# Window attention in front of a saturated TensorE: scores and products with v as float32 matmuls on parts of the array

## Chip, cores and metric

One core of a Trainium2 chip runs the whole program. The metric is device time in microseconds (us) of one execution. The profile's engines are PE (TensorE matmul), PEld (its weight loads), DVE (VectorE), ACT (ScalarE), POOL (GpSimd) and SP (SyncE, whose queue issues all DMAs here).

## What is computed

```python
# batch 8, heads 8, seq 576, head_dim 64; d_model 512, d_ff 2048; all inputs and the output float32
scores = scale * q @ k.T                       # masked to 0 <= i - j < 64
attn   = softmax(scores); a = attn @ v         # per batch and head
x      = a laid out as (4608 tokens, 512)
h      = x @ w_in
out    = (max(h, 0) + log1p(exp(-abs(h)))) @ w_out
```

Every token attends to itself and the 63 tokens before it.

## The kernel before, in words

The 4608 tokens are cut into 12 blocks of 384 (`TB`). In each block, attention is done for four pairs of heads (`hp`), and then the feed-forward part runs over 16 slices `f` of 128 of the 2048 inner columns. One step of the feed-forward part is an "up" (`ffn_up`, 12 matmuls at L390 into a bank `ps_h`, of which there are two) and a "down" (`ffn_down`, 9 matmuls at L411 into three accumulating banks `ps_o`). Matmul operands there are float32r pairs: a rounded part and the remainder, three products for each exact one. After an up, ACT takes abs, exp and ln (L394 to L396) and DVE adds the positive part and splits the result (L398 to L401).

`attention(g, hp)` is a generator. Each `yield` ends a stage, and the tables `STG0` (blocks 0 and 1) and `STG` (later blocks) give each stage a place on a common scale on which step n has its up at 2n + 0.5 and its down at 2n + 5.5. All events are sorted by that place. PE executes them exactly in this order (`MANUAL`); the other engines get their order from a scheduler, and each then works through its own queue in order. In later blocks a new pair of heads begins every 8 places, so every four feed-forward steps.

There are two kinds of attention:

- Blocks 0 and 1 (`by_pe`, eight pairs of heads) use plain float32. The scores of 128 queries for both heads come from one matmul against a block-diagonal tile `kbd` (L263). The probabilities are turned by PE (L303), and the products with v (L352) are 12 matmuls, 64 columns of v as the weight and 64 queries streamed, first the six of one head, then the six of the other; the two heads write different halves of the output's partitions.
- The ten later blocks (40 pairs) split q and k into float32r parts on ACT and DVE (L241, L242, L247, L248): the scores take 4 matmuls for 128 queries (L267). The probabilities are split into two float16 parts `nat`, turned by two transposing DMAs into `tr` (L311). v is split into three bfloat16 parts (L331 to L335), and 18 matmuls for each head (L364) multiply. DVE and ACT add the two halves of the result (L370, L371) and split it into `x` (L373, L374).

The scores cover 192 keys for 128 queries; the first and the last 64 columns hold a query's window in the upper and the lower half of the partitions. L274 scales, masks and takes the minimum, and L280 folds the last 64 columns onto the first. ACT takes exp (L284), and L293 and L295 normalise. Attention's banks are three `ps_a`.

At the start, the weights arrive as raw words and are rebuilt by ACT and DVE (`load_w`, L176 to L183), while attention of the first blocks runs beside it.

Of the kernel before, what the change touches and what calls it, by code (L numbers as in the profile page):

```python
# [17 lines left out]
P = 128  # L18
# [13 lines left out]
STG = (-13, -5.9, -5, 0, 1, 2, 3, 4, 5, 6, 7, 7.1, 12, 14, 16, 17)  # L32
# [11 lines left out]
def window_attention_softplus_ffn(  # L44
# [70 lines left out]
    W = CH + P  # L115

    kbd_s = [att.tile([P, 2, CH + TB], F32, name="kbd", tag=f"k{i}") for i in range(2)]
    for t in kbd_s:  # L120
        nc.vector.memset(t[D:P, 0, :], 0.0)
        nc.vector.memset(t[0:D, 1, :], 0.0)
        nc.vector.memset(t[0:D, 0, 0:CH], 0.0)
        nc.vector.memset(t[D:P, 1, 0:CH], 0.0)

    v3z = cpool.tile([P, 2, NJ, 2, 2, D], BF16, name="v3z")
    v_ts = [att.tile([P, 2, NJ, P], F32, name="v_t", tag=n) for n in ("nat", "tr")]
    for t in v_ts:
        nc.vector.memset(t[0:CH, 0, 0, :], 0.0)
# [4 lines left out]
    mask = cpool.tile([P, W], BF16, name="mask")  # L134
    nc.gpsimd.memset(mask, 0.0)
    nc.gpsimd.affine_select(
        out=mask, in_=mask, pattern=[[1, W]], compare_op=ALU.is_gt, fill=FAR, base=0, channel_multiplier=-1
    )
    nc.gpsimd.affine_select(
        out=mask, in_=mask, pattern=[[-1, W]], compare_op=ALU.is_ge, fill=FAR, base=CH, channel_multiplier=1  # L140
    )

    mask_c = cpool.tile([P, W], BF16, name="mask_c")
    nc.gpsimd.tensor_copy(mask_c, mask)
    nc.gpsimd.memset(mask_c[:, 0:CH], FAR)
    ident = att.tile([P, P], F32, name="ident", tag="xf")
    make_identity(nc, ident)

    mask_b = cpool.tile([P, W], BF16, name="mask_b")
    nc.gpsimd.tensor_copy(mask_b, mask)  # L150
    nc.gpsimd.memset(mask_b[CH:P, 0:P], FAR)
    nc.gpsimd.memset(v3z, 0.0)
# [3 lines left out]
    def load_w(f):  # L156


        if f < NE + 4:
            k = FIRST[f % 4] if f < NE else (4, 6)[f % 2]  # L160
            parts = [(spare(k, [P, 2, DM], w_words.dtype, "raws"), spare(k + 1, [P, 2, DM], F32, "ws"), 0, 2)]
        else:
            parts = [
                (
                    ff.tile([P, 1, DM], w_words.dtype, name="raw"),
                    att.tile([P, 1, DM], F32, name="wh", tag=("v_in", "v12")[m]),
                    m, m + 1,
                )
                for m in range(2)
            ]  # L170
# [18 lines left out]
    def attention(g, hp):  # L189
# [12 lines left out]
        heads = [slice(0, D), slice(D, P)]  # L202

        if by_pe:
            qf = ld.tile([P, 2, TB], F32, name="q_in") if hp % 2 else ld.tile([P, 2, W - P + TB], F32, name="k_in")
            qf = qf[:, 0, 0:TB]
            kf = kbd_s[hp % 2]
            skip = CH if t0 == 0 else 0
            nc.sync.dma_start(qf, qT[c0 : c0 + P, t0 : t0 + TB])
            for hh in range(2):  # L210
                nc.sync.dma_start(kf[heads[hh], hh, skip:], kT[c0 + hh * D : c0 + (hh + 1) * D, t0 - CH + skip : t0 + TB])
        else:
            q_in = ld.tile([P, 2, TB], F32, name="q_in")
            k_in = ld.tile([P, 2, W - P + TB], F32, name="k_in")
            ts, ks = slice(t0, t0 + TB), slice(t0 - CH, t0 + TB)
            for half in heads:
                nc.sync.dma_start(
                    q_in[half, :, :], qT[c0 : c0 + P, ts].rearrange("(h d) t -> d h t", h=2)
                )
                nc.sync.dma_start(  # L220
                    k_in[half, :, :], kT[c0 : c0 + P, ks].rearrange("(h d) t -> d h t", h=2)
                )
        yield

        if by_pe:
            v_t = v_ts[hp % 2]

            def load_v(rows, lay, j0, j1, start):
                n = rows.stop - rows.start
                src = v[start + j0 * P : start + j1 * P, c0 : c0 + P].rearrange("(j p) n -> p j n", p=P)  # L230
                nc.sync.dma_start(v_t[rows, lay, j0:j1, :], src[:n, :, :])

            if t0 == 0:
                nc.sync.dma_start(v_t[CH:P, 0, 0, :], v[0:CH, c0 : c0 + P])
            load_v(slice(0, P), 0, 1 if t0 == 0 else 0, NJ, t0 - CH)
            load_v(slice(0, CH), 1, 0, NJ, t0 + CH)
            load_v(slice(CH, P), 1, 0, NJ, t0)
        else:
            q_hl = att.tile([P, 2, TB], F32R, name="q_hl")
            low = heads[1]  # L240
            nc.scalar.copy(q_hl, q_in)  # L241
            nc.vector.tensor_tensor(  # L242
                q_hl[low, :, :], q_in[low, :, :], q_hl[low, :, :].bitcast(F32), ALU.subtract
            )
            yield
            k_hi, k_lo = [att.tile([P, 2, W - P + TB], F32R, name=f"k{i}") for i in range(2)]
            nc.scalar.copy(k_hi, k_in)  # L247
            nc.vector.tensor_tensor(k_lo, k_in, k_hi.bitcast(F32), ALU.subtract)  # L248
        yield

        if g == 0:

            st = spare(FIRST[hp], [P, 2, NJ, W], F32, "st0")
        else:
            st = att.tile([P, 2, NJ, W], F32, name="st", bufs=2)
        mn = att.tile([P, 2, NJ], F32, name="mn", bufs=2)
        sm = att.tile([P, 2 * NJ], F32, name="sm", bufs=2)
        for j in range(NJ):
            sp = bank()
            spv = sp[:, : 2 * W].rearrange("p (h c) -> p h c", h=2)  # L260
            js, kc = slice(j * P, (j + 1) * P), slice(j * P, j * P + W)
            if by_pe:
                mm(spv, qf[:, js], kf[:, :, kc], start=True, stop=True)  # L263
            else:
                for hh in range(2):
                    for i, part in enumerate((k_hi, k_lo)):
                        mm(  # L267
                            spv[:, hh, :], q_hl[:, hh, js], part[:, hh, kc],
                            start=(hh == 0 and i == 0), stop=(hh == 1 and i == 1), skip_group_check=True,
                        )  # L270
            t = ORDER[g] * NJ + j
            m = mask_c if (t * P) % S == 0 else mask_b if (t * P) % S + P > S else mask
            for hh in range(2):
                nc.vector.tensor_tensor_reduce(  # L274
                    st[:, hh, j, :], spv[:, hh, :], m, QSCALE, 3.0e38, ALU.add, ALU.min, mn[:, hh, j : j + 1]
                )
            yield

        sv = st.rearrange("p h j c -> p (h j) c")
        nc.vector.tensor_tensor(sv[:, :, 0:CH], sv[:, :, 0:CH], sv[:, :, P:], ALU.min)  # L280
        for hh in range(2):
            for j in range(NJ):
                i = hh * NJ + j
                nc.scalar.activation(  # L284
                    sv[:, i, 0:P], sv[:, i, 0:P], AF.Exp, bias=mn[:, hh, j : j + 1], scale=-1.0, accum_out=sm[:, i : i + 1]
                )
# [7 lines left out]
        pn = sv[:, :, 0:P]  # L294
        nc.vector.tensor_tensor(pn, pn, sm.unsqueeze(2).to_broadcast([P, 2 * NJ, P]), ALU.mult)  # L295
        if by_pe:

            yield
            pt = att.tile([P, 2, TB], F32, name="pt", tag="q_hl")
            for hh in range(2):  # L300
                pp = bank()
                for j in range(NJ):
                    tp(pp[:, j * P : (j + 1) * P], sv[:, hh * NJ + j, 0:P], ident)  # L303
                nc.scalar.copy(pt[:, hh, :], pp[:, :TB])
        else:
# [8 lines left out]
            nc.scalar.copy(nat[:, 0, :, :], pn)  # L314
            turn(0)
            yield
            nc.vector.tensor_tensor(nat[:, 1, :, :], pn, nat[:, 0, :, :], ALU.subtract)
            turn(1)
            yield
            v_in = att.tile([P, 2, NJ, P], F32, name="v_in")  # L320

            before, own = [v[t : t + TB, c0 : c0 + P].rearrange("(j p) n -> p j n", p=P) for t in (t0 - CH, t0)]
            nc.sync.dma_start(v_in[:, 0, :, :], before)
            nc.sync.dma_start(v_in[0:CH, 1, :, :], own[CH:P, :, :])
            nc.sync.dma_start(v_in[CH:P, 1, :, :], own[0:CH, :, :])
            yield

            v12 = att.tile([P, 2, NJ, 2, 2, D], BF16, name="v12")
            vv = v_in.rearrange("p u j (h d) -> p (u j h) d", h=2)
            v1, v2, v3 = [t.rearrange("p u j h i d -> p (u j h) i d")[:, :, i, :] for t, i in ((v12, 0), (v12, 1), (v3z, 0))]  # L330
            nc.scalar.copy(v1, vv)  # L331
            nc.vector.tensor_tensor(vv, vv, v1, ALU.subtract)
            yield
            nc.scalar.copy(v2, vv)
            nc.vector.tensor_tensor(v3, vv, v2, ALU.subtract)  # L335
# [8 lines left out]
        if by_pe:  # L344
            av = bank()
        else:
            xf = att.tile([P, TB], F32, name="xf")
        for hh in range(2):
            if by_pe:
                for a in range(2 * NJ):  # L350
                    cs = slice(a * CH, (a + 1) * CH)
                    mm(  # L352
# [159 lines left out]
```

## Time and profile before

| | |
|---|---|
| median of three runs | 1008.7 us (1007.8 to 1010.62) |
| the profiled execution, its span | 1013.1 us, 1011.3 us |
| PE matmul | 959.9 us, 6240 instructions |
| PE weight loads | 851.7 us |
| DVE | 730.4 us, 1689 instructions |
| ACT | 710.4 us, 1673 instructions |
| DMA queue of the program | 99.65 MB, 36.8% of 16 engines' span |

Busy time of PE is time in which some matmul is under way. A matmul's record begins at its start and ends when its results have left the array, so records of a stream overlap, and the pace of a stream is read from start to start, not from one record's length. A float32 matmul (L263, L352) leaves two weight loads and two matmul records; a float32r, bfloat16 or float16 one leaves one of each. In the chain of waits a piece's length is the time until the next piece takes over.

### The profile page before, as it was taken

The numbers are of one execution on the slowest core, as the hardware profiler recorded it, in microseconds if no ns is written. First come the engines' busy times: TensorE is split into PE (matmuls) and PEld (weight loads), VectorE is DVE, ScalarE is ACT, GpSimd is POOL, SyncE is SP. The second block draws the span as 40 slices with busy tenths as digits, with TensorE's granted clock in tenths as the row PEclk, the third lists the DMA queues.
The fourth block names the chain that finished last, engine by engine and source line by source line (L and its number), as shares of the span: only waits on it lengthen the run. The fifth ranks groups of instructions, "written<-read, shape, count | busy, mean of one in ns | idle before, by whom it ended". The sixth has DMA issues, their size and how long they took to land.

```text
span 1011.3 us, 17290 instructions
## 1 busy us (share of the span) xinstructions
PE 959.9 (95%) x6240; PEld 851.7 (84%) x6240; DVE 730.4 (72%) x1689; ACT 710.4 (70%) x1673; POOL 3.7 (0%) x14
## 2 busy tenths in 40 slices
PE   6546999999999999999999999999999999999998
PEld 3335888898988998899899998899889989998997
DVE  6897588787777777787777777777768867864332
ACT  4566678787777777777777677777767767865443
POOL 1000000000000000000000000000000000000000
PEclk9767999999999999999999999999999999999999
DMA  5845234443333434333334344433423423410000
GB/s 171 292 164 174 90 125 115 128 116 102 92 99 82 110 86 98 101 91 103 97 83 113 99 82 99 112 74 91 129 70 90 134 66 82 112 32 17 32 1 32
DMA packets 137238, 100.76 MB, mean 100 GB/s; under 512 B 70080, under 2 KB 129216, under 8 KB 135616
## 3 DMA queue, kind: packets, MB, share of 16 engines
q1 hardware_dynamic: 137152, 99.65, 36.8%
q8 instruction: 49, 0.80, 0.3%
q14 instruction: 37, 0.30, 0.1%
HBM read 73.66 MB, written 10.22 MB: 83 GB/s over the span
## 4 chain that ended last, share of the span: by engine, by line
PE 85%; DMA 6%; DVE 4%; ACT 4%; issue 1%; SPq 0%; ACTq 0%; DVEq 0%
PE ps_h L390 37%; PE ps_o L411 36%; PE ps_a L267 5%; PE ps_a L364 4%; DMA raws<-in_w_words_dram 3%; DMA raw<-in_w_words_dram 2%; ACT st L284 1%; DVE ws L178 1%; PE ps_a L263 1%; ACT ws L176 1%; PE ps_a L352 1%; DVE w L183 0%; DVE st L295 0%; DMA k_in<-in_kT_dram 0%; DVE ws L179 0%
## 5 line engine op out<-in xcount | busy, mean ns | idle before, releaser
L390 PE MATMUL ps_h<-x,w 128*128 128x384 f32 x2304 | 440.0, 339 | 0.6 <-ACT x L373 0.4
L411 PE MATMUL ps_o<-w,g 128*128 128x512 f32 x1728 | 433.9, 395 | 4.3 <-DVE g L401 3.1
L390 PEld LDWEIGHTS ps_h<-x,w 128*128 128x128 f32 x2304 | 404.7, 189 | 11.9 <-DVE u L398 1.0
L411 PEld LDWEIGHTS ps_o<-w,g 128*128 128x128 f32 x1728 | 319.5, 189 | 65.5 <-DVE g L401 5.2
L394 ACT ACTIVATE u<-ps_h 128x384 f32<-128x384 f32 x192 | 94.3, 491 | 198.3 <-PE ps_h L390 191.6
L398 DVE SCALAR_TENSOR_TENSOR u<-ps_h,u 128x384 f32<-128x384 f32 x192 | 106.9, 557 | 112.0 <-ACT u L396 109.3
L401 DVE TENSOR_TENSOR g<-u,g 128x384 fp32r<-128x384 f32 x192 | 106.3, 554 | 27.2 <-ACT g L400 25.9
L284 ACT ACTIVATE st<-st,mn 128x128 f32<-128x128 f32 x288 | 111.4, 388 | 9.4 <-DVE st L280 9.3
L274 DVE CUSTOM_DVE_ANT_0 st<-ps_a,mask 128x192 f32<-128x192 f32 x216 | 68.5, 351 | 50.5 <-PE ps_a L267 49.6
L395 ACT ACTIVATE u<-u 128x384 f32<-128x384 f32 x192 | 100.8, 525 | 4.4
L396 ACT ACTIVATE u<-u 128x384 f32<-128x384 f32 x192 | 100.2, 522 | 4.2
L400 ACT CAST g<-u 128x384 fp32r<-128x384 f32 x112 | 57.3, 512 | 31.9 <-DVE u L398 31.5
L267 PE MATMUL ps_a<-k,q_hl 128*128 128x192 f32 x480 | 76.6, 282 | 0.0
L267 PEld LDWEIGHTS ps_a<-k,q_hl 128*128 128x128 f32 x480 | 66.5, 191 | 3.2
L364 PEld LDWEIGHTS <-v 128*128 128x128 bf16 x960 | 44.1, 98 | 17.3 <-issue 17.3
L284 ACT ACTIVATION_READ_ACCUMULATOR st<-st,mn 128x1 f32 x288 | 53.8, 187 | 0.0
L364 PE MATMUL ps_a<-tr,v 128*128 128x64 f16 x960 | 53.6, 194 | 0.0
L364 PE MATMUL ps_a<-tr,v3z 128*128 128x64 f16 x480 | 50.4, 193 | 0.0
L295 DVE TENSOR_TENSOR st<-st,sm 128x768 f32<-128x768 f32 x48 | 45.9, 957 | 1.5
L371 DVE SCALAR_TENSOR_TENSOR xf<-ps_a,xf 64x384 f32<-64x384 f32 x80 | 43.8, 547 | 3.3 <-ACT xf L370 2.0
L248 DVE TENSOR_TENSOR k<-k_in,k 128x896 fp32r<-128x896 f32 x40 | 43.4, 1084 | 0.0
L364 PEld LDWEIGHTS <-v3z 128*128 128x128 bf16 x480 | 42.8, 98 | 0.0
(77 smaller groups left out, 762.2 us busy)
## 6 DMA issues: line engine op xcount, KB each, us to landing
k_in<-in_kT_dram SPq DMA_DIRECT2D x80, 224.0 KB, 3.6
q_in<-in_qT_dram SPq DMA_DIRECT2D x84, 192.0 KB, 3.9
raws<-in_w_words_dram SPq DMA_DIRECT2D x12, 1024.0 KB, 6.2
v_in<-in_v_dram SPq DMA_DIRECT2D x40, 192.0 KB, 2.6
v_in<-in_v_dram SPq DMA_DIRECT2D x80, 96.0 KB, 2.6
out_dram<-raw SPq DMA_DIRECT2D x12, 512.0 KB, 2.8
raw<-in_w_words_dram SPq DMA_DIRECT2D x8, 512.0 KB, 3.7
out_dram<-raw SPq DMA_DIRECT2D x12, 256.0 KB, 3.0
```

The source lines that it names most:

```text
L267: mm(spv[:, hh, :], q_hl[:, hh, js], part[:, hh, kc], start=(hh == 0 and i == 0), stop=(hh == 1 and i == 1), skip_group_check=True,)
L274: nc.vector.tensor_tensor_reduce(st[:, hh, j, :], spv[:, hh, :], m, QSCALE, 3.0e38, ALU.add, ALU.min, mn[:, hh, j : j + 1])
L284: nc.scalar.activation(sv[:, i, 0:P], sv[:, i, 0:P], AF.Exp, bias=mn[:, hh, j : j + 1], scale=-1.0, accum_out=sm[:, i : i + 1])
L364: mm(av[:, j * P + u * CH : j * P + (u + 1) * CH], w[:, u, j, hh, :, :], tr[:, s, hh * NJ + j, u * CH : (u + 1) * CH], start=(n == 0), sto ...
L390: mm(hv, weight(0, a, f)[:, c * P : (c + 1) * P], x[b][c], start=(i_mm == 0), stop=(i_mm == 3 * NC - 1))
L394: nc.scalar.activation(u, hv, AF.Abs)
L395: nc.scalar.activation(u, u, AF.Exp, scale=-1.0)
L396: nc.scalar.activation(u, u, AF.Ln, bias=1.0)
L398: nc.vector.scalar_tensor_tensor(gf, hv, 0.0, u, ALU.max, ALU.add)
L400: (nc.scalar.copy if g < 2 or f % 2 else nc.vector.tensor_copy)(gt[0], gf)
L401: nc.vector.tensor_tensor(gt[1], gf, gt[0].bitcast(F32), ALU.subtract)
L411: mm(ops[g][j], gt[a][:, js], weight(1, b, f), start=(first and i == 0), stop=(last and i == 2),)
```

## The change

The scores of all blocks become plain float32 matmuls on quarters of the array: 64 rows for a head's 64 dimensions, 64 columns for 64 queries, and 128 keys streamed. Each head has a bank of its own, the two halves of 128 queries go to the two halves of the partitions, and consecutive matmuls go to four different quarters. A query's 128 score columns now always hold its window, so the fold (L280) goes, and the mask is 128 wide. Splits of q, k and v go. In later blocks the two turned float16 parts are added by DVE into one float32 tile `pt`, and 12 float32 matmuls as in the first blocks multiply it with `v` as loaded, now alternating between the heads. The result is split straight from the bank. Each of q, k and v comes in one DMA (v overlapping with itself, 64 rows a step; block-first pieces take one more), into two buffers each.

```diff
-STG = (-13, -5.9, -5, 0, 1, 2, 3, 4, 5, 6, 7, 7.1, 12, 14, 16, 17)
+STG = (-13, -5, 0, 3, 4, 5, 6, 7, 13, 16)
...
+    heads = [slice(0, D), slice(D, P)]
+    halves = [slice(0, CH), slice(CH, P)]
...
+        q_in = ld.tile([P, TB], F32, name="q_in", bufs=2)
+        k_in = ld.tile([P, CH + TB], F32, name="k_in", bufs=2)
...
+        nc.sync.dma_start(q_in, qT[c0 : c0 + P, t0 : t0 + TB])
+        nc.sync.dma_start(k_in[:, skip:], kT[c0 : c0 + P, t0 - CH + skip : t0 + TB])
+        yield
+        v_in = att.tile([P, 2 * NJ, P], F32, name="v_in", bufs=2)
...
+        chunks = [[DM, P], [CH * DM, 2 * NJ - a0], [1, P]]
+        nc.sync.dma_start(v_in[:, a0:, :], bass.AP(v.tensor, v.offset + (t0 + (a0 - 1) * CH) * DM + c0, chunks))
+        yield
...
-            q_hl = att.tile([P, 2, TB], F32R, name="q_hl")
-            nc.scalar.copy(q_hl, q_in)
-            nc.vector.tensor_tensor(
-                q_hl[low, :, :], q_in[low, :, :], q_hl[low, :, :].bitcast(F32), ALU.subtract
-            )
...
-            nc.scalar.copy(k_hi, k_in)
-            nc.vector.tensor_tensor(k_lo, k_in, k_hi.bitcast(F32), ALU.subtract)
...
+        sps = [bank() for _ in heads]
         for j in range(NJ):
...
+            for u in range(2):
+                a = 2 * j + u
                 for hh in range(2):
-                    for i, part in enumerate((k_hi, k_lo)):
-                        mm(
-                            spv[:, hh, :], q_hl[:, hh, js], part[:, hh, kc],
-                            start=(hh == 0 and i == 0), stop=(hh == 1 and i == 1), skip_group_check=True,
-                        )
+                    mm(
+                        sps[hh][halves[u], js], q_in[heads[hh], a * CH : (a + 1) * CH],
+                        k_in[heads[hh], a * CH : (a + 2) * CH], start=True, stop=True,
+                    )
...
-            yield
+            if by_pe or j == NJ - 1:
+                yield
...
-        nc.vector.tensor_tensor(sv[:, :, 0:CH], sv[:, :, 0:CH], sv[:, :, P:], ALU.min)
...
-            nc.scalar.copy(v1, vv)
-            nc.vector.tensor_tensor(vv, vv, v1, ALU.subtract)
-            yield
-            nc.scalar.copy(v2, vv)
-            nc.vector.tensor_tensor(v3, vv, v2, ALU.subtract)
+            pt = att.tile([P, 2, TB], F32, name="pt")
+            nc.vector.tensor_tensor(
+                pt, *[tr[:, s, :, :].rearrange("p (h j) q -> p h (j q)", h=2) for s in range(2)], ALU.add
+            )
         yield
...
-            for n, (j, u, (w, s)) in enumerate(itertools.product(range(NJ), range(2), parts)):
-                mm(
-                    av[:, j * P + u * CH : j * P + (u + 1) * CH], w[:, u, j, hh, :, :],
-                    tr[:, s, hh * NJ + j, u * CH : (u + 1) * CH],
-                    start=(n == 0), stop=(n == 6 * NJ - 1), skip_group_check=True,
-                )
-            nc.scalar.mul(xf[ds, :], av[D:P, :TB], 1.0 / P_UNIT)
-            nc.vector.scalar_tensor_tensor(xf[ds, :], av[0:D, :TB], 1.0 / P_UNIT, xf[ds, :], ALU.mult, ALU.add)
...
+        av = bank()
+        for a, hh in itertools.product(range(2 * NJ), range(2)):
+            cs = slice(a * CH, (a + 1) * CH)
+            mm(
+                av[heads[hh], cs], v_in[:, a, heads[hh]], pt[:, hh, cs],
+                start=(a == 0), stop=(a == 2 * NJ - 1), skip_group_check=True,
+            )
+        unit = 1.0 if by_pe else 1.0 / P_UNIT
+        nc.scalar.mul(x_t[0], av[:, :TB], unit)
+        nc.vector.scalar_tensor_tensor(x_t[1], av[:, :TB], unit, x_t[0].bitcast(F32), ALU.mult, ALU.subtract)
```

In the changed kernel's numbering the scores' matmuls are L219, the reductions L226, the add into `pt` L272, the products L286, up L308, down L329, and the two DMA transposes L262.

Three places in the order of the instructions bear on what follows. On PE, in a late block, before: products of one head, then the scores of one third of a later pair's queries, with feed-forward work on both sides and two further such pieces in the same four steps.

```order
L364 LDWEIGHTS v_4259
L364 MATMUL ps_a<-tr,v_4259 128x64
L364 LDWEIGHTS v3z
L364 MATMUL ps_a<-tr,v3z 128x64
L267 MATMUL ps_a<-k_4240,q_hl 128x192
L267 MATMUL ps_a<-k_4241,q_hl 128x192
```

The same engine and place after the change, with the buffers' numbers:

```order
L329 MATMUL ps_o2_3111<-w11_88,g0_3139 128x512
L329 MATMUL ps_o2_3111<-w10_87,g1_3140 128x512
L286 MATMUL ps_a_3239<-pt_3186,v_in_2762 64x64 x12
L219 MATMUL ps_a_3257<-k_in_2952,q_in_2951 64x128
L219 MATMUL ps_a_3258<-k_in_2952,q_in_2951 64x128
```

All products of a pair and all scores of the pair two later now stand together, once in four steps.

On DVE around that place, after the change:

```order
L316 SCALAR_TENSOR_TENSOR u_3217<-ps_h_3204,u_3217 128x384
L272 TENSOR_TENSOR pt_3373<-tr_3192 128x768
L319 TENSOR_TENSOR g1_3223<-u_3217,g0_3222 128x384
L226 ISA st_3254,mn_3255<-ps_a_3257,mask_89 128x128
L226 ISA mn_3255 128x1
L292 SCALAR_TENSOR_TENSOR x1_1_1_3238<-ps_a_3239,x0_1_1_3237 128x384
L226 ISA st_3254,mn_3255<-ps_a_3258,mask_89 128x128
```

The `pt` that stands here (3373) is not the one that these products read (3186) but that of the next pair; it has one buffer, so it stands behind the products just named, and a whole pair's time ahead of its own.

On SP's queue, after the change, one pair's worth:

```order
L262 DMA_TRANSPOSE tr<-nat 128x6x128 x2
L203 DMA v_in<-in_v_dram 128x6x128
L193 DMA q_in<-in_qT_dram 128x384
L194 DMA k_in<-in_kT_dram 128x448
L262 DMA_TRANSPOSE tr<-nat 128x6x128 x2
```

Before, the same stretch held nine issues: two transposes, three pieces of v, two of k and two of q.

More of the change, by code (lines that the diff above doesn't have):

```diff
@@ L112, in weight @@
         return w_last[m, i, k][:, f % 4, :]
[L115 to L129, printed above, removed]
+    heads = [slice(0, D), slice(D, P)]
+    halves = [slice(0, CH), slice(CH, P)]
     FAR = BIG / QSCALE
-    mask = cpool.tile([P, W], BF16, name="mask")
+    mask = cpool.tile([P, P], BF16, name="mask")
     nc.gpsimd.memset(mask, 0.0)
-    nc.gpsimd.affine_select(
-        out=mask, in_=mask, pattern=[[1, W]], compare_op=ALU.is_gt, fill=FAR, base=0, channel_multiplier=-1
-    )
-    nc.gpsimd.affine_select(
-        out=mask, in_=mask, pattern=[[-1, W]], compare_op=ALU.is_ge, fill=FAR, base=CH, channel_multiplier=1
-    )
[L143 to L146, printed above, removed]
+    for i, half in enumerate(halves):
+        nc.gpsimd.affine_select(
+            out=mask[half, :], in_=mask[half, :], pattern=[[1, P]], compare_op=ALU.is_gt, fill=FAR,
+            base=0, channel_multiplier=-1,
+        )
+        nc.gpsimd.affine_select(
+            out=mask[half, :], in_=mask[half, :], pattern=[[-1, P]], compare_op=ALU.is_ge, fill=FAR,
+            base=CH, channel_multiplier=1,
+        )
+    mask_at = [cpool.tile([P, P], BF16, name=f"mask{i}") for i in range(2)]
+    for half, m in zip(halves, mask_at):
+        nc.gpsimd.tensor_copy(m, mask)
+        nc.gpsimd.memset(m[half, 0:CH], FAR)
+    ident = cpool.tile([P, P], F32, name="ident")
     make_identity(nc, ident)
[L149 to L152, printed above, removed]
     mm, tp = nc.tensor.matmul, nc.tensor.transpose
@@ L165, in load_w @@
                     ff.tile([P, 1, DM], w_words.dtype, name="raw"),
-                    att.tile([P, 1, DM], F32, name="wh", tag=("v_in", "v12")[m]),
+                    att.tile([P, 1, DM], F32, name="wh", tag=("nat", "tr")[m]),
                     m, m + 1,
@@ L200, in bank @@
             return ps_o.tile([P, 512], F32, name=f"ps_o{taken_ps[0] % NJ}")
[L202 to L218, printed above, removed]
-                )
-                nc.sync.dma_start(
-                    k_in[half, :, :], kT[c0 : c0 + P, ks].rearrange("(h d) t -> d h t", h=2)
-                )
@@ L223, in attention @@
-        yield
[L225 to L238, printed above, removed]
-            q_hl = att.tile([P, 2, TB], F32R, name="q_hl")
-            low = heads[1]
-            nc.scalar.copy(q_hl, q_in)
-            nc.vector.tensor_tensor(
-                q_hl[low, :, :], q_in[low, :, :], q_hl[low, :, :].bitcast(F32), ALU.subtract
-            )
-            yield
-            k_hi, k_lo = [att.tile([P, 2, W - P + TB], F32R, name=f"k{i}") for i in range(2)]
-            nc.scalar.copy(k_hi, k_in)
-            nc.vector.tensor_tensor(k_lo, k_in, k_hi.bitcast(F32), ALU.subtract)
+        q_in = ld.tile([P, TB], F32, name="q_in", bufs=2)
@@ new lines, in attention @@
+        k_in = ld.tile([P, CH + TB], F32, name="k_in", bufs=2)
+        skip = CH if t0 == 0 else 0
+        if skip:
+            nc.gpsimd.memset(k_in[:, 0:CH], 0.0)
+        nc.sync.dma_start(q_in, qT[c0 : c0 + P, t0 : t0 + TB])
+        nc.sync.dma_start(k_in[:, skip:], kT[c0 : c0 + P, t0 - CH + skip : t0 + TB])
+        yield
+        v_in = att.tile([P, 2 * NJ, P], F32, name="v_in", bufs=2)
+        a0 = 1 if t0 == 0 else 0
+        if a0:
+            nc.gpsimd.memset(v_in[0:CH, 0, :], 0.0)
+            nc.sync.dma_start(v_in[CH:P, 0, :], v[0:CH, c0 : c0 + P])
@@ L302, in attention @@
                 for j in range(NJ):
-                    tp(pp[:, j * P : (j + 1) * P], sv[:, hh * NJ + j, 0:P], ident)
+                    tp(pp[:, j * P : (j + 1) * P], sv[:, hh * NJ + j, :], ident)
                 nc.scalar.copy(pt[:, hh, :], pp[:, :TB])
@@ L313, in attention @@
             yield
-            nc.scalar.copy(nat[:, 0, :, :], pn)
+            nc.scalar.copy(nat[:, 0, :, :], sv)
             turn(0)
             yield
-            nc.vector.tensor_tensor(nat[:, 1, :, :], pn, nat[:, 0, :, :], ALU.subtract)
+            nc.vector.tensor_tensor(nat[:, 1, :, :], sv, nat[:, 0, :, :], ALU.subtract)
             turn(1)
             yield
[L320 to L333, printed above, removed]
-            nc.scalar.copy(v2, vv)
-            nc.vector.tensor_tensor(v3, vv, v2, ALU.subtract)
+            pt = att.tile([P, 2, TB], F32, name="pt")
+            nc.vector.tensor_tensor(
+                pt, *[tr[:, s, :, :].rearrange("p (h j) q -> p h (j q)", h=2) for s in range(2)], ALU.add
+            )
         yield
@@ L343, in attention @@
             xs[g][i][hp] = x_t[i]
[L344 to L352, printed above, removed]
-                        av[heads[hh], cs], v_t[:, a % 2, a // 2, heads[hh]], pt[:, hh, cs],
-                        start=(a == 0), stop=(a == 2 * NJ - 1), skip_group_check=True,
-                    )
-                if hh == 1:
-                    nc.scalar.copy(x_t[0], av[:, :TB])
-                    nc.vector.tensor_tensor(x_t[1], av[:, :TB], x_t[0].bitcast(F32), ALU.subtract)
-                yield
-                continue
-            av = bank()
-            parts = ((v12, 0), (v12, 1), (v3z, 0))
-            for n, (j, u, (w, s)) in enumerate(itertools.product(range(NJ), range(2), parts)):
-                mm(
-                    av[:, j * P + u * CH : j * P + (u + 1) * CH], w[:, u, j, hh, :, :],
-                    tr[:, s, hh * NJ + j, u * CH : (u + 1) * CH],
-                    start=(n == 0), stop=(n == 6 * NJ - 1), skip_group_check=True,
-                )
-            ds = heads[hh]
-            nc.scalar.mul(xf[ds, :], av[D:P, :TB], 1.0 / P_UNIT)
-            nc.vector.scalar_tensor_tensor(xf[ds, :], av[0:D, :TB], 1.0 / P_UNIT, xf[ds, :], ALU.mult, ALU.add)
-            if hh == 1:
-                nc.scalar.copy(x_t[0], xf)
-                nc.vector.tensor_tensor(x_t[1], xf, x_t[0].bitcast(F32), ALU.subtract)
-            yield
+        av = bank()
[4 more added lines that the diff above has]
+                start=(a == 0), stop=(a == 2 * NJ - 1), skip_group_check=True,
+            )
+        unit = 1.0 if by_pe else 1.0 / P_UNIT
+        nc.scalar.mul(x_t[0], av[:, :TB], unit)
+        nc.vector.scalar_tensor_tensor(x_t[1], av[:, :TB], unit, x_t[0].bitcast(F32), ALU.mult, ALU.subtract)
+        yield
     gs = {}
```

24 lines of the change are left out of this document (8 added, 16 removed).

## The prediction

> **What bounds the kernel now.** I read the page first, then the table by stretches of time, then the chain of waits in one steady stretch, then single records of the float32 matmuls. The page's engine line and its slices for PE:
>
> ```profile
> PE 959.9 (95%) x6240; PEld 851.7 (84%) x6240; DVE 730.4 (72%) x1689; ACT 710.4 (70%) x1673; POOL 3.7 (0%) x14
> PE   6546999999999999999999999999999999999998
> ```
>
> PE is idle only in the first 100 us. The table by stretches (busy time of PE, PEld, DVE, ACT, POOL, then PE's granted clock) shows why there are two regimes:
>
> ```profile
> 25.00:50.00 25.00, 13.02 (x74) 8.17 (x74) 21.66 (x64) 13.72 (x36) 0.00 (x0) 0.77 0.89 293
> 50.00:75.00 25.00, 10.79 (x66) 8.35 (x66) 24.51 (x46) 17.05 (x44) 0.00 (x0) 0.68 0.51 170
> 400.00:900.00 500.00, 500.00 (x3421) 450.67 (x3420) 379.63 (x892) 374.72 (x881) 0.00 (x0) 1.00 0.38 95
> ```
>
> At the start DVE is the full engine (21.66 and 24.51 of 25 us). From there on PE never stops, and DVE and ACT have a quarter of their time free. So in the steady part only PE's time counts. The chain of waits there, start and length of each piece:
>
> ```profile
> 396.75 2.10 PE ps_h L390 x12
> ...
> 403.04 2.09 PE ps_o L411 x9
> 405.13 0.54 PE ps_a L364 x18
> 405.67 0.51 PE ps_a L267 x4
> 406.17 2.13 PE ps_h L390 x12
> 408.31 0.54 PE ps_a L364 x18
> 408.85 0.51 PE ps_a L267 x4
> 409.36 2.10 PE ps_o L411 x9
> 411.45 0.42 PE ps_a L267 x4
> ...
> 416.08 2.10 PE ps_h L390 x12
> ...
> 960.54 2.10 PE ps_h L390 x12
> 962.64 2.08 PE ps_o L411 x9
> 964.72 2.10 PE ps_h L390 x12
> ```
>
> A pair of heads takes 416.08 - 396.75 = 19.33 us. Four feed-forward steps alone, as at the end, take 4 x (964.72 - 960.54) = 16.72. Attention therefore costs PE 2.61 us a pair, 40 times: 104 us. The pieces add up to 0.54 + 0.51 + 0.54 + 0.51 + 0.42 = 2.52; the rest is slightly longer pieces around them.
>
> **The float32 matmuls, priced from the first blocks.** The trace already holds the new kind of product (L352, one head after the other). First whole bursts, then what was in flight at single instants (start of the earliest record in flight, time to the end of the last, and how many):
>
> ```profile
> 21.42 1.43 PE L352 MATMUL ps_o<-pt,v_t 128*64 128x64 f32 x24 [0.83 <-ACT pt L304]
> 22.79 1.56 PE L263 MATMUL ps_o<-kbd,q_in 128*128 128x384 f32 x4
> 21.42 0.45 PE L352 MATMUL ps_o<-pt,v_t 128*64 128x64 f32 x4 [0.83 <-ACT pt L304]
> 21.94 0.45 PE L352 MATMUL ps_o<-pt,v_t 128*64 128x64 f32 x7
> 95.29 0.53 PE L352 MATMUL ps_a<-pt,v_t 128*64 128x64 f32 x3
> 96.04 0.59 PE L352 MATMUL ps_a<-pt,v_t 128*64 128x64 f32 x6
> 96.05 0.58 PE L352 MATMUL ps_a<-pt,v_t 128*64 128x64 f32 x5
> 97.27 0.31 PE L352 MATMUL ps_a<-pt,v_t 128*64 128x64 f32 x1
> ```
>
> 24 records in 22.79 - 21.42 = 1.37 us: 57 ns each, for 64 streamed columns at full clock. But within one head 3 or 4 are in flight, and where the second head begins 6 or 7 are, in both bursts. In the burst at 95 us a record takes 0.31 us and three span 0.53, so the first head's starts are (0.53 - 0.31) / 2 = 0.11 apart, twice the 57 ns (a lower clock). Its second record starts at 95.29, so the ninth at 95.29 + 7 x 0.107 = 96.04, and the second head's first starts at 96.05, when three of the first head's twelve have not begun. So the two halves of the columns run side by side, and a waiting matmul on one half lets a later one on the other half pass. Alternating heads should then take half: 24 x 29 ns. That is also the closest pace the trace shows for a weight load with its matmul (0.54 us for 18 in L364: 30 ns).
>
> The Trainium skill says otherwise ("TensorE: Matmul & The Clock Gate", Part 3, The mechanism): matmuls keep strict order with no passing, and weight loads overlap running matmuls only where the group of rows differs. By that rule the new scores, whose two records on one quarter stand next to each other, would come out as the first rival below. The rows at 96.04 and 96.05 speak against it.
>
> What it costs to leave full-array matmuls for such a burst, and to return, stands around an isolated one:
>
> ```profile
> 106.60 0.34 PE L390 MATMUL ps_h<-x,w 128*128 128x384 f32 x1
> 106.87 0.91 PE L352 MATMUL ps_a<-pt,v_t 128*64 128x64 f32 x12
> 107.71 0.44 PE L390 MATMUL ps_h<-x,w 128*128 128x384 f32 x1
> 107.99 0.34 PE L390 MATMUL ps_h<-x,w 128*128 128x384 f32 x1
> ```
>
> From 106.60 to 107.99 are 1.39 us. Two ups' matmuls at 2.10 / 12 = 0.175 and 12 records at 57 ns explain 1.03; 0.35 is the detour.
>
> **The change, part by part, steady blocks.**
> - Removed on PE: 2.61 us a pair.
> - Products (L286): 12 matmuls, 24 records. Between 24 x 29 = 0.70 us and 24 x 57 = 1.37. I take 0.70, since the overlap is in the trace.
> - Scores (L219): 12 matmuls, 24 records of 128 columns, so up to 114 ns each on its quarter (twice 57). One after the other: 2.74 us. Four quarters at once: 24 x 29 = 0.69. No run here shows two groups of rows at work at once, only two of columns. I take 0.70: consecutive matmuls go to different quarters, each row group has its own bank, and the pace is what two column halves reach already.
> - By the Trainium skill ("TensorE: Matmul & The Clock Gate", Part 3, Measured speedup against the span model) row tiles do run together: four of them gained 3.07 times. No run here shows it.
> - The detour: one a pair, since the order puts products and scores together: 0.35. Between the two stands another change of shape, from 128 rows to 64; between 0 and 0.35, I take 0.2, nearer the half detour (0.17). The last score records are longer than the products' (0.05).
> - Sum: 0.70 + 0.70 + 0.35 + 0.2 + 0.05 = 2.0 us instead of 2.61, so 0.6 less. In block 2 the new order still keeps products and scores apart, with a second detour: 0.3 less. 36 x 0.6 + 4 x 0.3 = 23 us.
>
> DVE and ACT, from the table of groups (number, then busy us, mean ns):
>
> ```profile
> L242 DVE TENSOR_TENSOR q_hl<-q_in,q_hl 64x768 fp32r<-64x768 f32 x40 | 38.2, 955 | 1.4 <-ACT q_hl L241 0.2
> L248 DVE TENSOR_TENSOR k<-k_in,k 128x896 fp32r<-128x896 f32 x40 | 43.4, 1084 | 0.0
> L332 DVE TENSOR_TENSOR v_in<-v_in,v 128x768 f32<-128x768 f32 x40 | 38.2, 955 | 2.4 <-ACT v L331 2.4
> L335 DVE TENSOR_TENSOR v3z<-v_in,v 128x768 bf16<-128x768 f32 x40 | 38.1, 953 | 0.1
> L371 DVE SCALAR_TENSOR_TENSOR xf<-ps_a,xf 64x384 f32<-64x384 f32 x80 | 43.8, 547 | 3.3 <-ACT xf L370 2.0
> L280 DVE TENSOR_TENSOR st<-st 128x384 f32<-128x384 f32 x48 | 26.5, 553 | 0.1
> L295 DVE TENSOR_TENSOR st<-st,sm 128x768 f32<-128x768 f32 x48 | 45.9, 957 | 1.5
> L317 DVE TENSOR_TENSOR nat<-st,nat 128x768 f16<-128x768 f32 x40 | 38.1, 952 | 0.9 <-ACT nat L314 0.9
> L284 ACT ACTIVATE st<-st,mn 128x128 f32<-128x128 f32 x288 | 111.4, 388 | 9.4 <-DVE st L280 9.3
> ```
>
> A late pair loses 0.96 + 1.08 + 0.96 + 0.95 + 2 x 0.55 + 0.55 = 5.6 us on DVE and gains the add into `pt` (0.95, as L317, also 768 wide with a float16 source). The six reductions shrink from 192 to 128 columns; a column costs (957 - 553) / 384 = 1.05 ns, so 0.07 each, 0.4 in all. DVE: 5 us less of about 15. ACT loses four conversions of q, k and v and two readings of the result. All this lies beside PE's work and is worth nothing in the steady part.
>
> What the new waits hold up: `pt` has one buffer, so on DVE the next pair's add waits until the present products are done, and behind it queue a split of g, the reductions and the x remainder. It waits about 1 us, once a pair, and is a whole pair early; PE's reader is not late. On SP the load of `v` waits for the products two pairs back (two buffers); q, k and the two transposes stand behind it, but these are wanted only after the next normalisation, some 7 us after those products, and the four issues fewer per pair leave SP emptier. The costs are nothing, unless DVE's queue grows too long: the second rival.
>
> **The start.** Here DVE counts. In eight pairs L280 goes (8 x 0.55 = 4.4) and 48 reductions shrink (3.4): 8 us. PE's scores were cold and slow:
>
> ```profile
> 4.55 3.89 PE ps_a L263 x6
> ```
>
> Six records, 3.89 us on the chain. At 107 ns for 64 columns, as in the burst at 95 us, 24 records of 128 take 24 x 214 / 4 = 1.3 us if four run at once, 5.1 if none do. Not all of it lies on the chain, which also waits for weights by DMA. Between 0 and 15 us less, I take 7, near the DVE term.
>
> **The sum.** 23 + 7 = 30 us off the profiled execution, 1013.1 to 983. That execution lies 4.4 above the median of the runs, so against 1008.7: 979 us.
>
> **Rivals.**
> - Only two of four at once. If a quarter's second record blocks all behind it, each score matmul takes 114 ns and the scores 1.39 instead of 0.70. Then a pair costs 2.7, 0.1 more than now (4 us), less some 4 from the start: 1009. For it: nothing in the trace shows row groups side by side. Against it: the passing at 96.05.
> - DVE's queue becomes the bound. From the start of the products: they end after about 1 us, then on DVE add 0.95, split 0.55, x remainder 0.55, six reductions 1.7, to 4.8; the last exps (six at 388 ns, partly beside) to 6; normalise 1.3 to 7.3; ACT's float16 copy 0.8 and DVE's remainder 0.95 to 9.1; then the positive part of the next up, 0.55, which frees its bank: 9.6. The third up after the burst needs that bank at 2.0 + 2 x 4.18 = 10.4. So 0.8 us is spare. Each us beyond it costs 36; at 1.4 us longer the gain is gone, at 2 longer than assumed (1.2 beyond the spare) it is 979 + 43 = 1022, slower than before. For it: these links were spread over more places before. Against: the pieces have measured lengths.
> - No overlap at all. Products 1.37, scores 2.74, detours 0.6: 4.7 a pair, 2.1 more, 40 times 84 us: 1090. Against it: the instants with 6 and 7 in flight.
>
> **Chances.** The forecast 0.69; two of four 0.17; DVE's queue 0.08; no overlap 0.06. A difference under 0.3% (3 us) can't be told from none here. The forecast's own range: downwards, the change of shape between the bursts may cost nothing (36 x 0.2 = 7), the detour half as much (36 x 0.17 = 6), and the start may give 8 more: 958. Upwards, the start gives nothing (7) and the detours cost 0.3 more (11): 997. The range must take in the first rival: 958 to 1013 leaves out the last and most of the second. Faster 0.77 (the forecast, a third of the first rival), same 0.07, slower 0.16.
>
> **What would show it.** In the profile after: in the steady part one burst of 24 products and 24 scores every 18.7 us, about 2.0 us from the down before it to the up behind it; starts of products about 29 ns apart and up to 8 in flight; PE without idle time, DVE at half and ACT under 60%; some 6380 PE records; an earlier first slice with PE at 9. Scores 57 ns apart would be the first rival; idle PE ahead of an up, released by DVE, the second; idle PE ahead of the products, released by the add into `pt`, would mean that I misread whose `pt` it is. What would make all this wrong at once is a detour that grows with the number of quarters in use.

## The result and the profile after

The changed kernel takes 1132.29 us (median; 1131.05 to 1134.57), the kernel before 1008.93. The ratio is 1.1231, with a 95% interval of 1.121 to 1.1252: 123 us slower, where 30 us faster was forecast. The profiled execution took 1133.0 us.

The engine line, and the slices of PE and of its granted clock, from the page of the changed kernel:

```profile
PE 1006.9 (89%) x6384; PEld 864.2 (76%) x6384; DVE 552.5 (49%) x1431; ACT 579.7 (51%) x1433; POOL 3.9 (0%) x23
PE   5449899998999899989998999899989999899998
PEclk9989999999999999998999999999998999999999
```

DVE and ACT are half empty, as forecast, and PE has its 6384 records. But PE now has slices with an 8 all along. The table by stretches (busy time of PE, PEld, DVE, ACT, POOL, then PE's granted clock) and the table of groups for PE between 250 and 900 us (busy, mean ns, idle time before and its releaser) say how much, and at which line:

```profile
400.00:900.00 500.00, 455.94 (x2908) 392.63 (x2907) 232.66 (x628) 249.27 (x622) 0.00 (x0) 0.95 0.23 64
```

```profile
L308 PE MATMUL ps_h<-x,w 128*128 128x384 f32 x1368 | 288.6, 364 | 0.0
L329 PE MATMUL ps_o<-w,g 128*128 128x512 f32 x1025 | 258.6, 396 | 0.0
L219 PE MATMUL ps_a<-k_in,q_in 64*64 64x128 f32 x696 | 57.3, 295 | 57.9 <-DVE mn L226 57.9
L286 PE MATMUL ps_a<-pt,v_in 128*64 128x64 f32 x696 | 26.6, 226 | 0.0
```

PE was busy for 500.00 of these 500 us before, now for 455.94. All of the idle time stands before one group: the scores, and what ends it is DVE's reduction at L226. There are 29 pairs between 250 and 900 us (696 records, 24 a pair), so each loses 57.9 / 29 = 2.0 us. The chain of waits over one pair, and a piece of the next:

```profile
414.03 0.87 PE ps_a L286 x24
414.90 0.02 issue
414.92 0.96 DVE pt L272
415.88 0.47 DVE g L319
416.35 0.20 DVE st L226
416.55 0.01 DVE mn L226
416.56 0.47 DVE x L292
417.03 0.20 DVE st L226
...
417.29 0.50 PE ps_a L219 x6
417.79 0.27 DVE st L226
...
418.13 0.65 PE ps_a L219 x8
418.78 2.30 PE ps_h L308 x12
...
435.76 0.87 PE ps_a L286 x24
...
440.54 3.79 PE ps_h L308 x12
```

Before, this chain held nothing but PE. Now DVE stands between the products and the second third of the scores, with exactly the instructions that stood in the order: the add into `pt`, a split of g, a reduction, the x remainder, a reduction. PE's own side of the same stretch in the timeline (in brackets the idle time before and its releaser):

```profile
414.80 0.45 PE L219 MATMUL ps_a<-k_in,q_in 64*64 64x128 f32 x8
416.61 0.43 PE L219 MATMUL ps_a<-k_in,q_in 64*64 64x128 f32 x2 [1.36 <-DVE mn L226]
417.29 0.44 PE L219 MATMUL ps_a<-k_in,q_in 64*64 64x128 f32 x6 [0.25 <-DVE mn L226]
418.13 0.65 PE L219 MATMUL ps_a<-k_in,q_in 64*64 64x128 f32 x8 [0.40 <-DVE mn L226]
```

The first 8 records (the first 128 queries, both heads) start right behind the products. The next two wait 1.36 us. Both heads' banks, `sps`, are now taken once for all three thirds, and the code writes four matmuls into them, then two reductions that read them, then four matmuls again. So head 0's scores of the second third wait until DVE has reduced head 0's first third, and DVE first has to do what stands ahead in its queue. By the code these scores go to other columns than the reduction reads (`js` differs), but the bank is the same, and the wait in the trace is for that reduction. Before, each third took a bank of its own.

The chain above shows a second loss: the up at 418.78 takes 2.30 us, that at 440.54 takes 3.79. Between 250 and 900 us, 19 of the 29 ups behind a burst take 3.6 to 3.85. The table by stretches, twice two stretches in a row: around a slow up, from 395.56 to 399.31, and around the one at 418.78, which is not slow:

```profile
392.58:395.99 3.41, 1.95 (x19) 1.28 (x20) 2.33 (x14) 1.92 (x9) 0.00 (x0) 1.00 0.41 115
395.99:399.41 3.42, 3.42 (x12) 3.42 (x11) 1.45 (x5) 0.89 (x5) 0.00 (x0) 0.50 0.41 125
413.06:416.47 3.41, 2.19 (x37) 1.43 (x35) 2.11 (x4) 1.52 (x3) 0.00 (x0) 1.00 0.04 11
416.47:419.89 3.42, 2.63 (x23) 1.96 (x24) 1.79 (x13) 2.60 (x12) 0.00 (x0) 1.00 0.36 106
```

In the second line PE is busy throughout, and its granted clock is 0.50. The idle time in the burst thus costs a second time, about 1.45 us (3.75 against 2.30).

Why some ups and not others can be read from these stretches. Between 250 and 900 us the clock stands at 0.50 in 19 stretches. Each is 3.41 us long, and they begin 44.4 or 23.9 us apart, which is 13 or 7 times 3.41: in this trace the clock changes on a fixed beat of 3.41 us. What counts, by and large, is how much idle time falls into one beat. Ahead of the 19 slow ups one beat holds 1.29 to 2.00 us of it (first line: 3.41 - 1.95 = 1.46). In the ten other pairs a boundary divides the gaps, and the fuller beat holds 1.14 to 1.33 (third line: 1.22).

A pair takes 22.77 us on average over these 29 (the up behind the first burst starts at 259.02, that behind the last at 896.54, 28 pairs between), against 19.33 before: 3.44 us more. In blocks 3 to 11, 34 of the 36 pairs have a later pair's scores right behind their products (the last two have none), and 34 x 3.44 = 117 of the 123 us. The other 6 lie outside these bursts; what the first three blocks gain and lose was not taken apart.

### The profile page after: what moved, and what is told of

The parts are those of the page before. It is cut to its first block, busy times and chain, and to the rows that moved or that the text cites. A ratio compares the mean times of both kernels' runs of the same rounds, so it can differ in the third digit from the quotient of the medians.

```text
span 1131.2 us, 16632 instructions
## 1 busy us (share of the span) xinstructions
PE 1006.9 (89%) x6384; PEld 864.2 (76%) x6384; DVE 552.5 (49%) x1431; ACT 579.7 (51%) x1433; POOL 3.9 (0%) x23
## 4 chain that ended last, share of the span: by engine, by line
PE 80%; DVE 11%; DMA 5%; ACT 2%; issue 1%; POOL 0%; POOLq 0%; ACTq 0%; SPq 0%; DVEq 0%
PE ps_h L308 38%; PE ps_o L329 34%; PE ps_a L219 5%; DMA raws<-in_w_words_dram 4%; PE ps_a L286 3%; DVE pt L272 3%; DVE st L226 2%; DVE g L319 2%; DVE x L292 1%; DMA raw<-in_w_words_dram 1%; ACT ws L162 1%; DVE w L169 0%; DVE ws L165 0%; DVE ws L164 0%; ACT st L236 0%
## 5 line engine op out<-in xcount | busy, mean ns | idle before, releaser
L308 PE MATMUL ps_h<-x,w 128*128 128x384 f32 x2304 | 476.0, 359 | 0.0
L308 PEld LDWEIGHTS ps_h<-x,w 128*128 128x128 f32 x2304 | 439.5, 203 | 20.8 <-issue 7.3
L329 PE MATMUL ps_o<-w,g 128*128 128x512 f32 x1728 | 437.0, 397 | 0.0
L329 PEld LDWEIGHTS ps_o<-w,g 128*128 128x128 f32 x1728 | 326.8, 191 | 61.4 <-DVE g L319 0.4
L219 PE MATMUL ps_a<-k_in,q_in 64*64 64x128 f32 x1104 | 93.3, 315 | 106.1 <-DVE mn L226 102.3
L219 PEld LDWEIGHTS ps_a<-k_in,q_in 64*64 64x64 f32 x1104 | 47.6, 140 | 144.2 <-DVE mn L226 134.5
L226 DVE CUSTOM_DVE_ANT_0 st<-ps_a,mask 128x128 f32<-128x128 f32 x276 | 71.3, 286 | 49.7 <-PE ps_a L219 49.4
L268 DVE TENSOR_TENSOR nat<-st,nat 128x768 f16<-128x768 f32 x40 | 38.3, 958 | 51.0 <-ACT nat L265 51.0
L286 PEld LDWEIGHTS ps_a<-pt,v_in 128*64 128x64 f32 x1104 | 38.9, 143 | 21.6 <-issue 15.9
L265 ACT CAST nat<-st 128x768 f16<-128x768 f32 x40 | 33.1, 827 | 40.5 <-issue 40.5
L286 PE MATMUL ps_a<-pt,v_in 128*64 128x64 f32 x1104 | 46.0, 232 | 4.6 <-ACT pt L255 3.8
L272 DVE TENSOR_TENSOR pt<-tr 128x768 f32<-128x768 f16 x40 | 38.3, 958 | 23.0 <-PE ps_a L286 21.7
```

Of the source, the lines that this page charges most:

```text
L219: mm(sps[hh][halves[u], js], q_in[heads[hh], a * CH : (a + 1) * CH], k_in[heads[hh], a * CH : (a + 2) * CH], start=True, stop=True,)
L226: nc.vector.tensor_tensor_reduce(st[:, hh, j, :], sps[hh][:, js], m, QSCALE, 3.0e38, ALU.add, ALU.min, mn[:, hh, j : j + 1])
L286: mm(av[heads[hh], cs], v_in[:, a, heads[hh]], pt[:, hh, cs], start=(a == 0), stop=(a == 2 * NJ - 1), skip_group_check=True,)
L308: mm(hv, weight(0, a, f)[:, c * P : (c + 1) * P], x[b][c], start=(i_mm == 0), stop=(i_mm == 3 * NC - 1))
L329: mm(ops[g][j], gt[a][:, js], weight(1, b, f), start=(first and i == 0), stop=(last and i == 2),)
```

## The experiments

Theory: the loss is PE waiting inside the scores for DVE's readers of the same bank; the rest of the prediction (parts of the array side by side, the price of the detour) holds. Rivals: the add into `pt`, held back by its single buffer, is what costs; the parts of the array do not run side by side, or the small matmuls themselves, and not the idle time, bring the clock down. In the kernels with the first edit below, line numbers move by 1 to 4: scores L215 (or L216), reductions L224, products L284 (L285), up L306 (L307), down L327 (L328).

**Scores first.** All 12 matmuls of the scores are written ahead of the six reductions, into the same two banks; nothing else changes.

```
+for a, hh in itertools.product(range(2 * NJ), range(2)):
+    mm(sps[hh][halves[a % 2], a // 2 * P : (a // 2 + 1) * P],
+       q_in[heads[hh], a * CH : (a + 1) * CH], k_in[heads[hh], a * CH : (a + 2) * CH], ...)
 for j in range(NJ):
     js = slice(j * P, (j + 1) * P)
-    for u in range(2):
-        a = 2 * j + u
-        for hh in range(2):
-            mm(sps[hh][halves[u], js], ...)
     ...
     for hh in range(2):
         nc.vector.tensor_tensor_reduce(...)
```

> All twelve score matmuls of a pair are issued before the first of its six reductions; nothing else differs from the changed kernel. Theory A (the loss is PE waiting, inside the score burst, for DVE to finish reading the same bank, and the lower clock that follows this idle time): the 102 us of waits of L219 for L226 vanish, no up takes 3.7 us any more, a steady pair takes 16.7 + 0.87 (products) + about 0.7 (scores, 18 ns a record as within the first third now) + 0.25 = 18.5 us instead of 22.8, and the time falls by about 165 us to 965 to 985, below the kernel before. Rival B (the matmuls on quarters themselves bring the clock down or cost a long drain): the waits go, but two of three ups after a burst stay at 3.7 us; time 1010 to 1040. Rival C (the add into pt, which stands ahead of the reductions on DVE, is the cause, wherever it stands): PE idles somewhere else for DVE, time above 1050.

Measured: 970.22 us (968.4 to 971.43), ratio to before 0.9613 (0.9578 to 0.9647). That is 162 us less than the changed kernel and 39 less than the kernel before; it beats both. Its engine line and PE's slices, and the chain:

```profile
PE 923.6 (95%) x6384; PEld 813.6 (84%) x6384; DVE 539.1 (56%) x1431; ACT 564.1 (58%) x1433; POOL 3.9 (0%) x23
...
PE   5458989999999999999999999999999999999998
```

```profile
401.12 0.85 PE ps_a L284 x24
401.97 0.81 PE ps_a L215 x24
402.79 2.31 PE ps_h L306 x12
...
419.76 0.85 PE ps_a L284 x24
420.61 0.81 PE ps_a L215 x24
421.42 2.28 PE ps_h L306 x12
...
438.35 0.85 PE ps_a L284 x24
```

DVE has left the chain; a pair takes 438.35 - 419.76 = 18.59 (18.64 the one before). No up between 250 and 900 us is slow any more (2.31 and 2.28 here), with the same small matmuls: so it was the idle time that brought the clock down. What the scores do is seen in the timeline at two single instants, 60 and 290 ns into a burst (start of the earliest record in flight, time to the end of the last, and how many):

```profile
420.54 0.34 PE L215 MATMUL ps_a<-k_in,q_in 64*64 64x128 f32 x4
420.54 0.56 PE L215 MATMUL ps_a<-k_in,q_in 64*64 64x128 f32 x12
```

60 ns into the burst four records are in flight, and after 290 ns twelve: by the order three for each of the four quarters. So four quarters do run side by side, and the rival on the parts of the array falls, for this order.

**Two buffers for `pt`,** in the changed kernel, the scores left as they are. The add then no longer waits for the products, and stands on DVE before them.

```
-pt = att.tile([P, 2, TB], F32, name="pt")
+pt = att.tile([P, 2, TB], F32, name="pt", bufs=2)
```

> Only a second buffer for pt, so that DVE's add of the next pair no longer stands behind the present products and ahead of the reductions; scores and reductions alternate as in the changed kernel. Theory A: of the 2.0 us of idle PE in a pair, the 1.0 us that the add takes goes, the rest stays, since the x remainder and the reductions are still waited for; 40 us less at least, more if the shorter idle keeps the clock up: 1050 to 1095. Rival C (the add is the whole cause): the waits of L219 vanish and the time falls below 1000.

Measured: 1074.17 us (1073.23 to 1074.78), ratio 1.0643 (1.0607 to 1.068). From the table of waits over the whole execution (us, times, longest), the changed kernel and then this one, and this one's timeline of PE:

```profile
PE ps_a L219 <- DVE mn L226: 102.3, 125, 4.7
PE ps_a L219 <- DVE mn L226: 69.5, 125, 4.5
```

```profile
424.42 0.45 PE L219 MATMUL ps_a<-k_in,q_in 64*64 64x128 f32 x8
425.28 0.43 PE L219 MATMUL ps_a<-k_in,q_in 64*64 64x128 f32 x2 [0.41 <-DVE mn L226]
425.95 0.44 PE L219 MATMUL ps_a<-k_in,q_in 64*64 64x128 f32 x6 [0.25 <-DVE mn L226]
426.79 0.65 PE L219 MATMUL ps_a<-k_in,q_in 64*64 64x128 f32 x8 [0.40 <-DVE mn L226]
```

The first gap falls from 1.36 to 0.41, by the length of the add (0.96), the other two stay. With 1.06 us of gaps in a pair, 5 of the 31 ups behind a burst between 250 and 900 us are still slow (3.48 to 3.66 us): each time all three gaps lie in one beat of the clock, 1.05 us in it (one more beat with as much was not followed by the low clock). The add into `pt` is thus part of the cause, and with the clock more than a third of the loss against scores first (58 of 162 us), but without it PE still waits, and the kernel is still slower than before.

**Both edits.** If the add mattered by itself, two buffers would help here too.

> As e1_scores_first with a second buffer for pt as well. If PE no longer waits for DVE anywhere in a steady pair (theory A): the same time as e1_scores_first within 0.3%, 967 to 973. If the add into pt still costs anything there (rival C): up to 0.96 us x 40 = 38 us faster.

Measured: 970.44 us (968.27 to 972.89), ratio 0.9617 (0.9596 to 0.9638): the same as scores first alone. The single buffer costs something only where PE waits for DVE behind the add.

These three split the loss per pair. Changed kernel to scores first: 22.77 - 18.61 = 4.16 us; in 34 bursts that is 141 of the 162 us measured, and the rest lies in the first three blocks, whose scores waited for DVE too. With two buffers a pair whose up is not slow takes 20.78 (20.75 and 20.81 for two neighbouring ones), so the waits that have nothing to do with `pt` are 20.78 - 18.61 = 2.17: 1.06 idle, the rest because short pieces, each with its own run-out (the tail of its last records), don't overlap as one burst does (0.45, 0.43, 0.44 and 0.65 in the rows above, 1.97 us in all, against 0.81). The add ahead of them is 0.96. The clock is 19 / 29 x 1.45 = 0.95. Together 4.1. On average, slow ups included, the pair of two buffers takes 20.98 (31 ups from 259.75 to 889.05).

**Products head after head,** with scores first: is the alternation of heads worth anything?

```
-for a, hh in itertools.product(range(2 * NJ), range(2)):   # products
+for hh, a in itertools.product(range(2), range(2 * NJ)):
```

> As e1_scores_first, but the products of a pair run first all of one head, then all of the other, instead of alternating. If alternating is what halves them (theory): the burst of 24 records takes 1.37 us as in the first blocks of the kernel before, instead of 0.87, 0.5 us more in 40 pairs: 20 us (2%) slower than e1_scores_first. If the two column halves overlap anyway by passing: no difference.

Measured: 990.81 us (989.16 to 991.72), ratio 0.9816 (0.9782 to 0.9851), 20.6 us more than scores first. The chain:

```profile
405.67 1.36 PE ps_a L284 x24
407.04 0.82 PE ps_a L215 x24
```

The 24 records take 1.36 us instead of 0.85; 0.51 x 40 = 20. Two halves of the columns run side by side if consecutive matmuls alternate.

**Products and scores apart,** with scores first: the last entry of the stages' table goes from 16 to 18, so that a feed-forward step stands between them and a pair has two detours.

```
-STG = (-13, -5, 0, 3, 4, 5, 6, 7, 13, 16)
+STG = (-13, -5, 0, 3, 4, 5, 6, 7, 13, 18)
```

> As e1_scores_first, but the products come two places later, so that one step's matmuls stand between scores and products and PE leaves the full array twice in a pair. The prediction's terms: a detour costs 0.35 us, the change of shape between the two bursts 0.2; so 0.15 us more in 40 pairs, 6 us. If changing from 128 to 64 rows costs nothing: 0.35 x 40 = 14 us. If the detour costs less than an isolated burst showed: nothing.

Measured: 976.49 us (975.23 to 978.65), ratio 0.9678 (0.9636 to 0.9719), 6.3 more than scores first. The chain has the long up twice:

```profile
401.47 0.81 PE ps_a L215 x24
402.29 2.31 PE ps_h L306 x12
404.60 2.09 PE ps_o L327 x9
406.69 0.85 PE ps_a L284 x24
407.54 2.31 PE ps_h L306 x12
```

**The order of the scores' quarters,** with scores first. Three kernels: (a) one half of the columns after the other, the two heads' rows alternating; (b) one head's rows after the other, the column halves alternating; (c) one quarter after the other.

```
-for a, hh in itertools.product(range(2 * NJ), range(2)):
+for u, j, hh in itertools.product(range(2), range(NJ), range(2)):  # (a), a = 2 * j + u
+for hh, a in itertools.product(range(2), range(2 * NJ)):           # (b)
+for hh, u, j in itertools.product(range(2), range(2), range(NJ)):  # (c), a = 2 * j + u
```

(a) 

> As e1_scores_first (all scores ahead of the reductions), but in another order of the twelve score matmuls: first all that write the upper half of the partitions, the two heads (the two row halves of the array) taking turns, then all that write the lower half. Theory (quarters work independently, two at once here): 24 records of about 110 ns, two at a time, 1.3 us and a tail of 0.2 instead of 0.81, so 0.7 us a pair, 28 us (2.9%) slower than e1_scores_first. If row halves do not overlap (what the prediction could not see): 2.6 us, 75 us slower. If matmuls pass each other far enough ahead: less than 28.

(b) 

> As e1_scores_first, but head after head: the two column halves of the array take turns within one head's rows. Theory: the same 1.5 us as with the rows in turn, about 28 us slower than e1_scores_first. If the two kinds of half differ, this one, whose kind of overlap the kernel before showed, is the faster.

(c) 

> As e1_scores_first, but quarter after quarter, three score matmuls (six records) on one quarter before the next. Theory: 24 records of about 110 ns one after the other, 2.6 us and a tail, 2.0 us a pair, 80 us slower than e1_scores_first, less what the next quarter overtakes at each of the three changes (three or four records each, up to 1 us a pair): 40 to 80 us. Strict order with full overlap by the array alone would give the whole 80.

Measured: (a) 982.58 (979.02 to 983.46), (b) 973.86 (972.93 to 977.05), (c) 998.71 (996.78 to 1000.04); ratios 0.974 (0.9723 to 0.9756), 0.9656 (0.9635 to 0.9677), 0.9895 (0.9878 to 0.9912). The bursts of (a), (b) and (c) in their chains:

```profile
402.76 1.08 PE ps_a L216 x24
```

```profile
417.53 1.08 PE ps_a L215 x24
```

```profile
406.90 1.62 PE ps_a L216 x22
```

All three expectations were too high. (a) and (b) were to cost 28 us each over scores first and cost 12 and 4; their bursts are equal and 0.27 longer, which makes 11. So the 9 us between them do not come from the steady part. In the profiled executions, 4.2 us apart in span (977.2 and 973.0), the same step's up starts at 374.57 in (a) and at 370.44 in (b): those 4 us are there before 375 us. Where they arise, and the rest of the 9, was not found. (c) was to cost 40 or more and cost 28: the burst is 0.81 longer, 32 us. The reason is the passing that the prediction read from the burst at 95 us. Three matmuls on one quarter give six records some 0.11 us apart, and while those wait for their quarter, the next quarter's overtake: in the burst of (c) that begins at 406.83 three records have begun by 407.100 and a fourth by 407.106, too soon behind the third to be on the same quarter. Records strictly one after the other would make 24 x 0.108 = 2.6 us; even the worst order takes 1.62. So order within a burst matters far less than what a burst has to wait for.

## Why the prediction was wrong

- **What the new waits hold up: the step that failed.** It read "the costs are nothing, unless DVE's queue grows too long". It asked who waits for the add into `pt`, and named what queues behind it on DVE: a split of g, the reductions, the x remainder. It did not ask who waits for those reductions. In the steady part before, PE did not wait for DVE at all (its 500.00 busy us of 500), because each third's scores had a bank of its own. The edit moves `sps` out of the loop, and with that the reduction of one third stands ahead of PE's matmuls of the next. The pieces to price it were all there: add 0.95, split 0.55, reduction about 0.28 stand on DVE between the end of the products and the first release, 1.8 us, and less the first piece of 0.45 that is about the gap of 1.36 us.
- **The rival on DVE's queue (0.08)** named the right engine and the wrong place: it followed the queue to the third up's bank, with 0.8 us to spare. The up never waited for DVE (0.0 idle before L308). The wait came before it, in the burst itself. Its condition was a queue that is too long; what counted was only the order of its first three entries. It gave 1022, so even there the size would have been wrong.
- **What the idle time costs in clock** was not in the prediction at all: 0.95 of the 4.16 us a pair.
- **Column halves and quarters side by side: right.** 0.85 and 0.81 us for the two bursts, with the run-in in them. The Trainium skill's rule that matmuls keep strict order with no passing ("TensorE: Matmul & The Clock Gate", Part 3, The mechanism) would give 1.39 for the scores, as in the prediction's first rival, and between 2.3 and 2.6 for (c) (an estimate: records 0.108 apart, with or without overlap where the quarter changes); the runs gave 0.81 and 1.62. The measurements decide against the rule for these float32 matmuls. The alternating products decide nothing here: strict order would let each head's next matmul begin beside the other's, for about the same 0.7 (an estimate, 12 x 57 ns).
- **Detour and change of shape: right in sum.** In scores first attention costs 18.61 - 16.72 = 1.89 us a pair, where 2.0 was forecast. The terms make up for each other: the bursts take 1.66 where 1.45 was put, and the up behind them 0.2 more than others, where detour and change of shape were put at 0.55. Two detours instead of one with a change of shape cost 6.3 / 40 = 0.16 more a pair.
- **DVE's and ACT's load: right, and beside the point.** DVE went from 730.4 to 552.5 us. A mean share of 49% says nothing on how long a given reader takes to get its turn.
- **The start: too small, and not shown by an experiment of its own.** Scores first is 38.7 us faster than before; 0.72 x 36 = 26 of it is the steady part, so about 13 are left for the first three blocks, where 8 were forecast (7 for the start, 1 for block 2). The issue of the first write of `part`, which ends the first piece of block 0 (the kernel before, the changed kernel, scores first, from their timelines), comes 5.4 us earlier in the changed kernel and 15.6 earlier in scores first; 15.6 and 26 are together the difference of the two spans (1011.3 - 969.6 = 41.7):

```profile
116.48 1.05 SPq L431 DMA_DIRECT2D part<-raw  x2
111.04 1.05 SPq L349 DMA_DIRECT2D part<-raw  x2
100.89 1.06 SPq L347 DMA_DIRECT2D part<-raw  x2
```

- **Two slips in its sums** bear on nothing above: the last rival adds up to 1008.7 + 84 = 1093, not 1090, and its chances give about 0.75 for faster, not 0.77.

Had the reductions been written behind all the scores, the prediction's own sum, 979, would have been met by 970: close, but with a steady part made up of terms that traded places and a start that gave more than was put.

Not tried: a bank for each head and third with the interleaved order; that takes six banks, and there are three `ps_a` for the scores and the output.

## What to carry to other kernels

When a change puts several pieces into one buffer that had one each, ask for every writer which reader it now waits for, even where the two touch different columns, and read the order on that reader's engine from the moment the buffer is written: the wait is the sum of what stands there, however empty the engine is on average. If pieces share a buffer, write all of them first and read afterwards; on TensorE this also keeps small matmuls in one burst, where parts of the array overlap. Price a gap on TensorE twice, once as idle time and once for the clock behind it.

## What the runs showed of the hardware that was not expected

- Gaps of 1.36, 0.25 and 0.40 us within 4 us were enough to bring the granted clock to 0.50 for the next up in 19 of 29 pairs; gaps of 0.41, 0.25 and 0.40 did so in 5 of 31. The Trainium skill describes both a re-throttle after gaps of more than about 3.4 us ("TensorE: Matmul & The Clock Gate", Part 1, HAM oscillation) and a swinging clock from short idles between groups of matmuls (same page, Part 1, A second HAM failure mode). The trace agrees with the second: no single gap of these bursts came near 3.4 us. Between 250 and 900 us the clock stayed low for one beat of 3.41 us each time, so a burst with the same gaps is hit or spared by where it falls on the beat. Idle time alone gives no sharp limit: beats with 1.05 us of it (two buffers) were followed by the low clock, and beats with up to 1.33 (changed kernel) were not. What else counts stays open.
- Four float32 matmuls on different quarters begin so close that all four are in flight 60 ns into a burst, and each quarter takes its next record 0.11 us later: 12 in flight at once, where up to 8 were expected.
- An order that gives one quarter all its matmuls first still gets 1.62 us instead of 2.6, since later quarters pass those that wait.
